# Full-array key-value products, TensorE transposes of one batch, and a new instruction order in a gated-linear-attention and MLP-mixer kernel

## The chip, the cores and the metric

The kernel runs on one core of a Trainium2 chip. A core has TensorE (PE in the profile; its weight loads are listed apart as PEld), VectorE (DVE), ScalarE (ACT), GpSimd (POOL) and SyncE (SP, which here only issues DMAs). TensorE writes into PSUM, which has eight banks; SBUF holds all other tiles. The metric is device time in microseconds of one execution, and the comparison is between medians of runs.

## What is computed

Four batches, eight heads, 768 tokens, 48 channels per head. First a recurrent linear attention with a decay per channel, then an MLP mixer over tokens and channels (384 channels, that is 8 x 48):

```python
for t in range(S):
    state = alpha[:, :, t, :, None] * state + np.einsum('bhd,bhe->bhde', k[:, :, t], v[:, :, t])
    y[:, :, t] = np.einsum('bhd,bhde->bhe', q[:, :, t], state)
...
xt = x.transpose(0, 2, 1)
h = np.maximum(xt @ w_tok1, 0.0) @ w_tok2
u = x + h.transpose(0, 2, 1)
h2 = np.maximum(u @ w_ch1, 0.0) @ w_ch2
return (u + h2).astype(np.float32)
```

Here x is y with the heads laid side by side: 768 tokens by 384 channels per batch.

## The kernel before

**Attention in chunks.** `attention(n)` (L126) handles one chunk of 256 tokens of one batch, for all eight heads; n runs from 0 to 11, and n = 3b + k is chunk k of batch b. A chunk's tokens lie as 128 partitions by two neighbouring tokens (the index s). Four loads of 384 KB bring alpha, k, q and v (`ld_at`, `ld_kt`, `ld_qt`, `ld_vt`, L138 to L142). Logarithms of alpha (ln, ln1, lnP; ACT) are summed over tokens on PE (cum, or cumw for the first three chunks) and turned into factors E and IE by exponentials (ACT). kk and qq (L170, L172) scale k and q by them into bf16 tiles pkk and pkq; vb (L174) casts v. For n of 3 and more, P, k0a, q0r and r1 first fold the two tokens of a partition.

trk and trq transpose pkk and pkq on PE (n below 6; copied out of PSUM by evk and evq), or dk and dq do it by DMA transposes issued on SP (n from 6), with pq reordering the result. G0 and G1 (`gmm`, L657) are the masked products of keys and queries inside each half chunk, 16 small products each on 48 rows by 64 columns of the array; mask0 and mask1 (DVE) bring them out. Half hf means the tokens on partitions 64 hf to 64 hf + 63.

**K.** The key-value product K (L205, `kmm`, L678) gives, for each half chunk, the sum over its tokens of key times value, for all heads. It works on 64 x 64 quarters of the array: for each pair of heads j, each s, each half hf and each head r of the pair, one product of 64 tokens with 48 moving columns; the two s accumulate in PSUM. That is 32 products, or 16 for the last chunk of a batch (k = 2), whose second half state nobody needs. The result holds one head of a pair in partitions 0 to 63 and the other in 64 to 127. `sfirst`, `sadd` (sa0, sa1) and `smul` (sm0, sm1) turn it into the running state, reading it twice (`twice`, L692) against a factor that is zero off the block diagonal. After K, vs0 and vs1 (`vswap`, L674) write v of the other token over the other half's partitions in vb, so that afterwards vb[:, hf] holds all 128 tokens of half hf. ia and ib (`inter`) then multiply q with the state before, y0 and y1 (`ymm`) add the products inside the half, and x0 and x1 copy the result to x tiles.

**Mixer.** `mixer(b)` (L247) runs once all six x tiles of a batch are there: t1 (`tok1`, two banks of six products; for batch 0 product by product as x tiles come, for the others six at a time, L254 to L264), ht (ReLU), t2 (`tok2`), u (add, DVE), the transposition of u, c1 (`ch1`, 24 steps of three products of 384 columns), rt (ReLU, on ACT or DVE), c2 (`ch2`, six tiles of 12 products in four steps), o (add u, DVE) and st (store). u is transposed by PE for batch 0 (up and ut, L281 to L289) and by two DMA transposes on SP for the other batches (ux, L290 to L296). The weights come in 16 pieces of 384 KB (`ldw_`), and each is cast to bf16 (`cw_`): wt1 and wt2 in two pieces each, wc1 and wc2 in six each. A c1 step of mc 6 to 11 needs pieces 3 to 5 of wc1, one of mc 0 to 5 needs pieces 0 to 2.

**The order.** Nothing is scheduled at run time by the kernel itself. `ORDER` (L337) lists every operation once, by name, with a last letter for its engine (t PE, s ACT, v DVE, g POOL, y SP); each engine works through its own in that order, and each waits for what it needs. `BUFS` gives the buffer number of each value, `CLASSES` (L103) the number of buffers of each kind. The cost figures and due times in `build` (L113) do not enter the program. Operations marked port=True on DVE and POOL wait for each other in the listed order where the engine changes (`shared`, L641). Loads may be issued from SP's queue or from ACT's, in turn with that engine's other work. The names f1_ and f3_ are fillers: one or three products of zeros of 512 columns (`fill`, L565), which are there only for the first three chunks.

Of the kernel before, what the change touches and what calls it, by code (L numbers as in the profile page):

```python
# [63 lines left out]
class Plan:  # L64
# [33 lines left out]
NX = 6  # L98
OFF = -1024.0
# [5 lines left out]
    "la": 2, "lf": 2, "E": 2, "IE": 2, "pkq": 2, "pkk": 2, "vb": 3,  # L105
    "tpk": 4, "tpq": 2, "gtm": 2, "tmp": 2, "ss": 5, "x": 12, "ht": 3, "u": 4, "ut": 2, "rt": 22, "o": 3,
# [6 lines left out]
def build(g):  # L113
# [12 lines left out]
    def attention(n):  # L126
# [70 lines left out]
        for hf in range(2):  # L197
# [7 lines left out]
        KO = O("K", {"PE": (276.0 if nst == 2 else 140.0, 420.0)}, 9.5, writes=[kp], reads=[pkk, vb], preds=[kk, vc] + fill("K", kp) + ([prev_s[1]] if prev_s and k > 0 and n > NB else []),  # L205
               emit=lambda e: g.kmm(kp, pkk, vb, nst), mode="G")
        before = prev_s if k > 0 else None
        states = [before]
        for hf in range(nst):
            s_, sp = V("ss"), states[-1]  # L210
            if sp is None:
                so = O(f"s{hf}_", dve(384), 10, writes=[s_], reads=[kp, E], preds=[KO, et],
                       emit=lambda e, s_=s_, hf=hf: g.sfirst(s_, kp, E, hf, wide))
            else:
                t_ = V("tmp")
                ad = O(f"sa{hf}_", dve(384), 10 + hf, writes=[t_], reads=[kp, sp[0]], preds=[KO, sp[1]],
                       emit=lambda e, t_=t_, hf=hf, s0=sp[0]: g.sadd(t_, kp, s0, hf))
# [3 lines left out]
        for hf, st in enumerate(states[:2]):  # L221
            yp, x = V("one"), V("x")
            vs = O(f"vs{hf}_", either(dve(384, True), act(384, True), {"POOL": (405.0, 440.0)}), 10, writes=[vb], reads=[vt],
                   port=True, preds=[KO, vc], emit=lambda e, hf=hf: g.vswap(e, vb, vt, hf))
            held = []
            if st:
                held.append(O(f"i{'ab'[hf]}", pe([96] * 4), 13, writes=[yp], reads=[tpq, st[0]], preds=[evq, st[1]],
                              emit=lambda e, hf=hf, st=st, yp=yp: g.inter(yp, tpq, st[0], hf)))
            yo = O(f"y{hf}_", pe([48] * 8), 14, writes=[yp], reads=[gtm, vb],
                   preds=[masks[hf], vs] + held + (fill("y", yp) if hf else []),  # L230
# [16 lines left out]
    def mixer(b):  # L247
# [4 lines left out]
        for m in range(NDT):  # L252
            bank, ht = V("one"), V("ht")
            if b == 0:  # L254
                prev = None
                for kc in range(NS):
                    o = P.op(f"t1_{b}_{m}_{kc}", pe([384]), m0 + 900 * m * sc + kc, writes=[bank], reads=[x[kc][0]],
                             preds=[x[kc][1], wl[("wt1", kc // 3)]] + ([prev] if prev else []),
                             emit=lambda e, m=m, kc=kc, bank=bank: g.tok1(bank, m, kc, x[kc][0]))
                    prev = o  # L260
            else:
                prev = P.op(f"t1_{b}_{m}", pe([384] * 6), m0 + 900 * m * sc, writes=[bank], reads=[v for v, _ in x],
                            preds=[o for _, o in x] + [wl[("wt1", p)] for p in range(2)],
                            emit=lambda e, m=m, bank=bank: [g.tok1(bank, m, kc, x[kc][0]) for kc in range(NS)])  # L264
            ho = P.op(f"ht_{b}_{m}", either(act(384), dve(384)), m0 + 1000 * m * sc, writes=[ht], reads=[bank],
                      preds=[prev], emit=lambda e, bank=bank, ht=ht: g.relu(e, g.hts(ht), bank))
            hts.append((ht, ho))
# [13 lines left out]
        if b == 0:  # L281
# [15 lines left out]
        for mc in range(NDC):  # L297
            rt = V("rt")
            ro = []
            for half in range(2):  # L300
                bank = V("one")
                o = P.op(f"c1_{b}_{mc}_{half}", pe([384] * 3), m0 + (4900 + 975 * mc + 487 * half) * sc, writes=[bank],
                         reads=[ut], preds=(uts[0:2 + half] if b == 0 else [uts[half]]) + [wl[("wc1", mc // 6 * 3 + p)] for p in range(3)],
# [5 lines left out]
        for i in range(NS):  # L309
            hold = 4000.0 if (i >= NS - 3 and b < B - 1) else 0.0  # L310
            bank, o_ = V("one"), V("o")
            prev = None
            for q4 in range(4):
                pp = []
                for mc in range(3 * q4, 3 * q4 + 3):
                    pp.append(rts[mc][1][i // 3])
                prev = P.op(f"c2_{b}_{i}_{q4}", pe([384] * 3), m0 + (16700 + 1950 * i + 487 * q4) * sc + hold,
                            writes=[bank], reads=[rts[mc][0] for mc in range(3 * q4, 3 * q4 + 3)],
                            preds=pp + [wl[("wc2", mc // 2)] for mc in range(3 * q4, 3 * q4 + 3, 2)] + ([prev] if prev else []),
                            emit=lambda e, i=i, q4=q4, bank=bank: g.ch2(bank, i, q4, rts))  # L320
            oo = P.op(f"o_{b}_{i}", dve(384), m0 + (16750 + 1950 * (i + 1)) * sc + hold, writes=[o_],
                      reads=[bank, us[i][0]], preds=[prev],
                      emit=lambda e, i=i, bank=bank, o_=o_: g.oadd(o_, bank, us[i][0], i))
            P.op(f"st_{b}_{i}", {"SP": (420.0, 420.0), "ACT": (374.0, 374.0)}, m0 + (16800 + 1950 * (i + 1)) * sc + hold, reads=[o_], preds=[oo],
                 emit=lambda e, i=i, o_=o_: g.store(e, o_, b, i), dma=("o", OUT_NS, 1000.0, 520.0))
# [15 lines left out]
ld_kt0s ld_at0y ld_vt0s ld_at1y f1_trq0t ld_kt1s ld_qt0y f3_cumw1t ld_qt1y f1_K0t f1_cumw0t f3_cumw0t f1_cumw1t  # L341
f3_trk0t ln0s ld_at2y ld_vt1s cumw0t f3_K0t IE0s f3_trq0t ln1s kk0g ld_at3s ld_kt2y cumw1t E0s Et0s IE1s qq0v trk0t
ldw_wt10y E1s evk0s ld_qt2s Et1s kk1v trq0t ld_kt3y f3_cumw2t vb0v evq0v qq1g K0t f3_trq1t vs0_0s vb1s s0_0v f1_G00t
ld_qt3y G0_0t sa1_0v f1_trq1t f1_trk1t vs1_0g mask0_0v sm1_0g ld_vt2s K1t ln2s trq1t trk1t P3g sa0_1v evq1s f1_G10t
# [483 lines left out]
```

## Time and profile before

| | |
|---|---|
| median of 3 runs | 169.35 us (168.55 to 169.62) |
| the profiled execution | 168.55 us |
| its span | 166.8 us |
| PE busy in the span | 158.8 us |
| DVE, ACT, POOL busy | 118.5, 88.8, 63.9 us |
| granted TensorE clock, mean | 0.997 |
| HBM read, written | 25.17 MB, 4.72 MB |

The profile is of one execution. A busy PE counts the whole passage of a product through the array, and products overlap; the distance from one product's start to the next is the better price of it. "Idle before" is time in which an engine waited, with the operation that released it. Times in a timeline count from the start of the span.

### The profile page before, as it was taken

The page shows a single profiled execution, that of the slowest core. Times are in us where ns is not written, and L with a number is a line of the kernel's source. Part 1 is how long each engine was busy: PE and PEld are TensorE (multiplying, and loading weights), DVE is VectorE, ACT ScalarE, POOL GpSimd, SP SyncE. Part 2 cuts the span into 40 slices and gives each one's busy share as a digit, 9 for nine tenths or more (in the row PEclk, how much of TensorE's full clock was granted, in tenths as well). Part 3 has the DMA queues.
Part 4 walks back from the last instruction along what each step waited for, and adds up shares of the span by engine and source line. Part 5 has one row for each costly group of instructions (what it writes and reads, how often), then busy time and mean ns, then how long its engine had stood idle before and what let it go on. Part 6 is the DMA issues. An engine that isn't in the chain of part 4 may idle for free.

```text
span 166.8 us, 4619 instructions
## 1 busy us (share of the span) xinstructions
PE 158.8 (95%) x1906; PEld 98.2 (59%) x1906; DVE 118.5 (71%) x208; ACT 88.8 (53%) x170; POOL 63.9 (38%) x68
## 2 busy tenths in 40 slices
PE   7969999889999999999899999999999999999991
PEld 2446565656566676565566676666566665665660
DVE  4059979889898869996998899892588463153522
ACT  3586978988678886735764842428602101641100
POOL 4139476296445661521646739436320000000000
PEclk9999999999999999999999999999999999999998
DMA  5999999999999999899999999489201186200213
GB/s 121 325 325 327 334 356 297 354 363 336 356 367 323 311 325 247 216 251 239 206 200 273 237 271 150 99 212 211 64 0 51 47 68 171 94 0 0 94 51 141
DMA packets 76757, 35.10 MB, mean 210 GB/s; under 512 B 70336, under 2 KB 75712, under 8 KB 76736
## 3 DMA queue, kind: packets, MB, share of 16 engines
q1 hardware_dynamic: 53168, 23.99, 58.5%
q10 hardware_dynamic: 23568, 10.82, 23.4%
q8 instruction: 15, 0.25, 0.7%
q14 instruction: 6, 0.05, 0.1%
HBM read 25.17 MB, written 4.72 MB: 179 GB/s over the span
## 4 chain that ended last, share of the span: by engine, by line
PE 76%; DMA 8%; DVE 6%; ACT 4%; issue 2%; SPq 1%; POOL 1%; DVEq 0%; ACTq 0%
PE ps L770 27%; PE ps L765 25%; PE ps L563 16%; DMA in<-in_q_dram 8%; PE ps L746 3%; PE ps L741 3%; PE ps L624 2%; DVE pkk L612 1%; ACT vb L654 1%; DVE o L774 1%; POOL tpq L655 1%; ACT tpq L654 1%; SPq L504 1%; DVE in L548 1%; DVE in L604 1%
## 5 line engine op out<-in xcount | busy, mean ns | idle before, releaser
L770 PE MATMUL ps<-wc,rt 128*128 128x384 bf16 x288 | 54.2, 326 | 0.1
L765 PE MATMUL ps<-ut,wc 128*128 128x384 bf16 x288 | 50.7, 326 | 0.7 <-DVE o L774 0.7
L736 ACT ACTIVATE rt<-ps 128x384 bf16<-128x384 f32 x52 | 23.5, 491 | 27.8 <-PE ps L765 27.6
L765 PEld LDWEIGHTS <-wc 128*128 128x128 bf16 x288 | 27.2, 98 | 18.4 <-issue 1.2
L770 PEld LDWEIGHTS <-rt 128*128 128x128 bf16 x288 | 26.7, 98 | 16.9 <-issue 0.3
L738 DVE TENSOR_SCALAR rt<-ps 128x384 bf16<-128x384 f32 x44 | 22.8, 551 | 15.5 <-PE ps L765 15.5
L670 DVE TENSOR_TENSOR gtm<-ps,mk 128x1024 bf16<-128x1024 f32 x24 | 28.8, 1220 | 3.6 <-PE ps L563 3.4
L774 DVE TENSOR_TENSOR o<-ps,u 128x384 f32<-128x384 f32 x24 | 13.1, 552 | 7.5 <-PE ps L770 7.4
L612 POOL TENSOR_TENSOR pkq<-in,E 128x768 bf16<-128x768 f32 x7 | 12.7, 1814 | 13.2 <-DVE in L608 7.1
L612 POOL TENSOR_TENSOR pkk<-in,IE 128x768 bf16<-128x768 f32 x7 | 12.7, 1814 | 10.7 <-ACT IE L596 5.2
L563 PE MATMUL ps<-zs 128*128 128x512 bf16 x51 | 15.5, 428 | 1.1 <-DVE zs L468 1.1
L654 ACT CAST vb<-in 64x384 bf16<-64x384 f32 (+1 forms) x24 | 14.5, 603 | 2.7 <-PE ps L563 2.0
L654 ACT CAST x<-ps 128x384 bf16<-128x384 f32 x18 | 8.3, 480 | 13.8 <-PE ps L563 12.6
L750 DVE TENSOR_TENSOR u<-ps,x 128x384 bf16<-128x384 f32 x24 | 12.4, 552 | 3.2 <-PE ps L746 3.1
L707 POOL TENSOR_TENSOR ss<-tmp,E 128x384 bf16<-128x384 f32 x10 | 8.4, 836 | 7.7 <-DVE vb L655 2.4
L703 DVE TENSOR_TENSOR tmp<-ps,ss 128x384 f32<-128x384 f32 x16 | 8.8, 552 | 1.9 <-PE ps L563 1.2
L746 PE MATMUL ps<-ht,wt 128*128 128x384 bf16 x48 | 9.8, 326 | 0.4 <-ACT ht L736 0.4
L612 DVE TENSOR_TENSOR pkq<-in,E 128x768 bf16<-128x768 f32 x5 | 4.8, 953 | 7.2 <-DMA in<-in_q_dram 7.1
L563 PEld LDWEIGHTS <-tpk 48*64 48x64 bf16 x384 | 6.3, 106 | 6.1 <-issue 4.9
L741 PE MATMUL ps<-x,wt 128*128 128x384 bf16 x48 | 9.6, 327 | 0.0
L563 PE MATMUL ps<-tpq,tpk 48*64 48x128 bf16 x384 | 9.1, 220 | 0.4 <-DVE u L750 0.2
L655 POOL COPY tpq<-tpk 128x1024 bf16<-128x1024 bf16 x5 | 6.7, 1339 | 5.8 <-PE ps L770 2.7
(85 smaller groups left out, 191.6 us busy)
## 6 DMA issues: line engine op xcount, KB each, us to landing
in<-in_moe_w_ch_dram SPq DMA_DIRECT2D x12, 384.0 KB, 6.4
in<-in_q_dram SPq DMA_DIRECT2D x10, 384.0 KB, 7.3
in<-in_alpha_dram SPq DMA_DIRECT2D x9, 384.0 KB, 6.5
in<-in_v_dram ACTq DMA_DIRECT2D x9, 384.0 KB, 6.3
in<-in_k_dram ACTq DMA_DIRECT2D x7, 384.0 KB, 5.8
out_dram<-o SPq DMA_DIRECT2D x13, 192.0 KB, 4.2
out_dram<-o ACTq DMA_DIRECT2D x11, 192.0 KB, 1.9
in<-in_k_dram SPq DMA_DIRECT2D x5, 384.0 KB, 6.9
```

The costliest lines, as they stand in the source:

```text
L563: return self.pe.matmul(out, lhsT=lhsT, rhs=rhs, start=start, stop=stop, skip_group_check=True)
L612: self.shared(self.eng[e].tensor_tensor(self.t(dst)[:, :, :, 0:D], self.t(src).rearrange("p h s d -> p s h d"), bass.AP(tensor=f.tensor, o ...
L654: return self.act.copy(d, s)
L670: self.nc.vector.tensor_tensor(self.t(gtm)[:, hf, :, :], self.pair(gp).rearrange("p a (j t) -> p (a j) t", t=128), bass.AP(tensor=m.tensor ...
L736: self.act.activation(d, s, AF.Relu)
L738: self.nc.vector.tensor_scalar_max(d, s, 0.0)
L741: self.pe.matmul(self.bank(bank)[:, 0:HD], lhsT=self.wt1[:, kc, m * 128 : m * 128 + 128], rhs=self.t(x), start=(kc == 0), stop=(kc == NS - 1))
L746: self.pe.matmul(self.bank(bank)[:, 0:HD], lhsT=self.wt2[:, kc, i * 128 : i * 128 + 128], rhs=self.t(hts[kc]), start=(kc == 0), stop=(kc = ...
L750: self.nc.vector.tensor_tensor(self.t(u)[:, i % 3], self.bank(bank)[:, 0:HD], self.t(x), ALU.add)
L765: self.pe.matmul(self.bank(bank)[:, 0:HD], lhsT=self.wc1[:, kc, mc * 128 : mc * 128 + 128], rhs=self.t(ut)[:, 3 * half : 3 * half + 3, kc, ...
L770: self.pe.matmul(self.bank(bank)[:, 0:HD], lhsT=self.t(rts[mc][0])[:, i * 128 : i * 128 + 128], rhs=self.wc2[:, mc, :], start=(mc == 0), s ...
L774: self.nc.vector.tensor_tensor(self.t(o), self.bank(bank)[:, 0:HD], self.t(u)[:, i % 3], ALU.add)
```

## The change

For chunks 3 to 11 (batches 1 to 3) K works on the whole array: `kfull` makes one product per pair of heads and half, over all 128 tokens of the half, with 128 stationary columns (two heads of 64) and 96 moving columns. That needs both tokens' keys of a half in one tile, as vs0 and vs1 give it for v; vs0 and vs1 now run ahead of K, and `kturn` copies the keys: ka and kb fill a new tile kt for half 1 (from both tokens of partitions 64 to 127), kc overwrites partitions 64 to 127 of pkk's first token by the other token of half 0, after trk (or dk) has read it. A last chunk of a batch needs kc and vs0 alone. The result holds 96 columns per pair, so the state steps read it directly.

u of batch 1 goes through PE (`UP`), as for batch 0, and no longer through DMA transposes. The first token products are single steps for all batches. The last tile of the last batch (`LAST`) is worked, added and stored in two halves of 192 columns. Some kinds have more buffers (E, IE, pkk, the new kt) and some fewer (x, rt, ss). `ORDER` and `BUFS` are new throughout; the second half's y filler, if any, stands ahead of ib instead of y1. There are 34 filler products instead of 51.

```diff
+KFN = 3
+LAST = (3, 0)
+UP = (0, 1)
...
-    "la": 2, "lf": 2, "E": 2, "IE": 2, "pkq": 2, "pkk": 2, "vb": 3,
-    "tpk": 4, "tpq": 2, "gtm": 2, "tmp": 2, "ss": 5, "x": 12, "ht": 3, "u": 4, "ut": 2, "rt": 22, "o": 3,
+    "la": 2, "lf": 2, "E": 3, "IE": 3, "pkq": 2, "pkk": 3, "vb": 3,
+    "tpk": 4, "tpq": 2, "gtm": 2, "tmp": 2, "ss": 4, "kt": 1, "x": 9, "ht": 3, "u": 4, "ut": 2, "rt": 20, "o": 3,
...
+        turned = n >= KFN
+        if turned:
+            vs = [vsw(hf, [vc]) for hf in range(2)]
+            kx, kp_in = None, [kk, vc, vs[0]]
+            if nst == 2:
+                kx = V("kt")
+                ka = shift("ka", 9, [kx], [pkk], [kk], lambda e: g.kturn(e, kx, pkk, 0))
+                kb = shift("kb", 9, [kx], [pkk], [kk], lambda e: g.kturn(e, kx, pkk, 1))
+                kp_in += [ka, kb, vs[1]]
+            kc = shift("kc", 9, [pkk], [], [kk, trk if n < NX else evk] + ([ka] if nst == 2 else []),
+                       lambda e: g.kturn(e, None, pkk, 2))
+            KO = O("K", pe([96] * (4 * nst)), 9.5, writes=[kp], reads=[pkk, vb] + ([kx] if kx else []),
+                   preds=kp_in + [kc] + ([prev_s[1]] if prev_s and k > 0 and n > NB else []),
+                   emit=lambda e: g.kfull(kp, pkk, kx, vb, nst))
...
-        if b == 0:
+        if b in UP:
             for p in range(3):
...
+            cuts = [(0, HD // 2), (HD // 2, HD)] if (b, i) == LAST else [(0, HD)]
...
+    def kturn(self, e, kx, pkk, part):
+        k = self.t(pkk)
+        d, s = ((self.t(kx)[0:64] if kx else None, k[64:128, 0]), (self.t(kx)[64:128] if kx else None, k[64:128, 1]),
+                (k[64:128, 0], k[0:64, 1]))[part]
+        self.copy(e, d[:, :, 0:D], s[:, :, 0:D])
+
+    def kfull(self, kp, pkk, kx, vb, nst):
+        vv = self.t(vb)
+        for hf in range(nst):
+            kk = self.t(kx) if hf else self.t(pkk)[:, 0]
+            for j in range(4):
+                self.mm(self.bank(kp, hf)[:, 96 * j : 96 * j + 96], kk[:, 2 * j : 2 * j + 2, :],
+                        vv[:, hf, 2 * j : 2 * j + 2, :], j == 0, j == 3)
```

Of the new order, the beginning, and the places that the prediction speaks of (the start of the old one stands at L338):

```
ld_at1s ld_at0y ld_qt0s ld_kt0y f1_G00t f3_cumw1t ld_qt1y f1_cumw1t ld_vt1y ld_kt1y f3_G00t f3_cumw0t ln0s ld_vt0s
f1_trq1t ln1s cumw0t cumw1t Et0s IE0s f1_trq0t ld_vt3y E0s kk0v Et1s E1s qq0v IE1s qq1v trq0t ld_at2y f1_trk0t evq0s
trk0t vb0v ld_qt2y evk0v kk1g K0t ld_at3s s0_0v f3_K1t ld_kt2s ld_kt3y sa1_0v vs0_0s trq1t ldw_wt10y sm1_0g G0_0t
vs1_0s G1_0t vb3s f3_trk1t mask1_0v ld_vt2y vb1s trk1t mask0_0v vs1_3s K1t ln2s vs1_1g evq1s sa0_1v vs0_1v cumw2t
...
t1_0_1_5t cw_wt21g trq3t ht_0_0v ht_0_1s ldw_wc11s sa1_3v cw_wc14g t2_0_0t ldw_wc10s t2_0_1t u_0_0v evq3s ld_kt5s
t2_0_5t cw_wc13g ln14s t2_0_3t u_0_1v t2_0_2t u_0_3v P5g ld_qt4y up_0_0t t2_0_4t u_0_2v ld_at6y u_0_5v up_0_1t lnP5s
cw_wc12g ld_qt5y u_0_4v ut_0_0s G0_3t ib3t ut_0_1v up_0_2t cw_wc15g mask0_3v cum5t ut_0_2s G1_3t c1_0_9_0t k0a4v
c1_0_8_1t IE5s ln15s mask1_3v E5s kk4g c1_0_8_0t rt_0_9_0s c1_0_11_1t rt_0_8_0s c1_0_6_1t r15s rt_0_11_1v y0_3t
cw_wc11s rt_0_8_1v y1_3t cw_wc10g ldw_wc20y trk4t x1_3s ldw_wc21y c1_0_7_0t kb4g r14s ld_vt4y c1_0_1_0t sm1_3g evk4s
...
c1_0_1_1t qq5g kc4g rt_0_1_1s rt_0_5_1v P6g trq5t vs1_4s rt_0_5_0v ld_at9y ld_at7s evq5v cw_wc24s kc5g vs0_4g ld_qt6y
c1_0_6_0t c2_0_4_0t c1_0_10_1t ia4t c2_0_0_0t cw_wc22v rt_0_6_0s y0_4t K4t rt_0_10_1v cw_wc23s vb6v c2_0_1_0t cw_wc25s
...
t1_1_0_5t ht_1_1v dq6y c2_0_3_0t c2_0_5_3t ht_1_0s ld_kt8s q0r7g t2_1_3t ld_qt9y cum7t ld_vt8s u_1_3v t2_1_2t IE7s
```

## What is predicted

> **What bounds the kernel now.** I read the page's busy times and chain first, then busy time by stretches of 10 us, then TensorE's (PE's) timeline, where the distance from one start to the next is the price of a step, then DVE, ACT and the landings of loads.
>
> ```profile
> PE 158.8 (95%) x1906; PEld 98.2 (59%) x1906; DVE 118.5 (71%) x208; ACT 88.8 (53%) x170; POOL 63.9 (38%) x68
> PE 76%; DMA 8%; DVE 6%; ACT 4%; issue 2%; SPq 1%; POOL 1%; DVEq 0%; ACTq 0%
> ```
>
> ```profile
> 10.00:20.00 10.00, 9.12 (x186) 5.47 (x183) 9.54 (x13) 8.03 (x14) 5.02 (x6) 1.00 1.16 330
> 30.00:40.00 10.00, 8.72 (x123) 5.67 (x122) 8.85 (x17) 8.96 (x16) 6.02 (x7) 1.00 1.07 360
> 110.00:120.00 10.00, 10.00 (x70) 6.05 (x67) 4.71 (x11) 6.37 (x15) 3.89 (x4) 1.00 0.87 167
> ```
> (columns: PE, weight load, DVE, ACT, POOL, clock, DMA, GB/s). PE is the bound, but not everywhere alike: up to 40 us it is full of fillers while DVE, ACT and DMA are at 8 to 10 tenths; later its work is real. The seam is the first channel product, c1, at 37.88, which follows the last u transposes taken out of PSUM:
>
> ```profile
> 36.66 1.08 DVE L655 COPY ut<-ps 128x768 bf16<-128x768 bf16 x2
> 37.88 1.30 PE L765 MATMUL ps<-ut,wc 128*128 128x384 bf16 x7
> ```
>
> From 37.88 to the end of the last product's turn, 163.23, PE's steps take 125.35 us. By usual start-to-start times (c1 and c2 0.4875 per three products, G 0.248, y 0.205, i 0.17, cum 0.29, transposes 0.445 per eight) 121.05 is work, 14 runs of quadrant steps cost 0.188 each = 2.65 beyond their work, and 1.65 is waiting: 0.28 at 67 us, 0.24 at 73 to 75, 0.90 at 79, 0.23 at 100. The largest:
>
> ```profile
> 78.07 1.14 PE L765 MATMUL ps<-ut,wc 128*128 128x384 bf16 x6
> 79.94 0.97 PE L765 MATMUL ps<-ut,wc 128*128 128x384 bf16 x5 [0.73 <-DVE o L774]
> ```
> ```profile
> 78.86 0.56 DVE L608 TENSOR_TENSOR in<-in,lf 128x384 f32<-128x384 f32 x1 [1.25 <-DMA in<-in_q_dram]
> ```
> DVE stood at q0r9, whose load was issued at 73.31 behind two DMA transposes of u on SP (ux, 1.39 and 1.40 us of issue) and landed at 78.77; the bank that c1 needed was freed behind it.
>
> **The sum, part by part.** It is made against the profiled execution: 168.55 us with a span of 166.8. It is the fastest of the three runs shown; the median, 169.35, is 0.8 above, so I add 0.8 at the end.
>
> *Key-value products.* The quadrant form and its surroundings:
>
> ```profile
> 50.44 0.65 PE L765 MATMUL ps<-ut,wc 128*128 128x384 bf16 x3
> 51.02 0.44 PE L563 MATMUL ps<-vb,pkk 64*64 64x48 bf16 x32
> 51.39 0.62 PE L624 MATMUL ps<-idn,pkk 128*128 128x128 bf16 x8
> ```
> ```profile
> 95.54 0.42 PE L563 MATMUL ps<-tpq,tpk 48*64 48x128 bf16 x16
> 95.79 0.42 PE L563 MATMUL ps<-vb,pkk 64*64 64x48 bf16 x32
> 96.04 0.43 PE L563 MATMUL ps<-tpq,tpk 48*64 48x128 bf16 x16
> ```
> Alone, K's 32 products take 0.37, and the three c1 ahead take 0.58, not 0.4875; between two G steps K takes 0.25. So a run of quadrant steps costs some 0.09 going in and 0.10 coming out, and K itself 0.27 (half of it 0.20, between 0.185 and 0.246). A full-array product of 96 columns is the i row: four in 0.17. New K: eight = 0.34, or four = 0.17. For K4 to K11 (five whole, three half) 2.21 replaces 1.95: +0.26. But runs after the first c1 go from 14 to 10 in the new order: -0.75. [...]
>
> *Copies.* 21 new half-tile copies; nearest rows:
>
> ```profile
> L654 ACT CAST vb<-in 64x384 bf16<-64x384 f32 x17 | 8.7, 510 | 2.7 <-PE ps L563 2.0 <-issue 0.4
> L655 POOL CAST vb<-in 64x384 bf16<-64x384 f32 x5 | 2.5, 501 | 7.2 <-DVE ss L707 4.0 <-DVE in L604 3.0
> L655 DVE CAST vb<-in 64x384 bf16<-64x384 f32 x2 | 0.7, 356 | 0.1
> ```
> 9 on ACT 4.6, 9 on POOL 4.5, 3 on DVE 1.1. Nothing of it is on PE, which hides it as long as K's place comes late enough. K now waits for them, and every product behind K on PE with it. The tightest is K4, just before c2_0_1_0: after q0r5 POOL has qq5 1.81, kc4 0.50, P6 1.00, kc5 0.50, vs0_4 0.50 = 4.3 us to do, and the order leaves 4.6 us of PE work for it. Price: 0 to 1, in the waits below.
>
> *u of batch 1 by TensorE.* 18 transposes, three steps of 0.345 = +1.03 on PE, all on the path. Three copies out (DVE 0.56 twice, ACT 0.82) lie beside products of c2_0. Gone are two DMA transposes and SP's 2.8 us. ld_qt9 moves ahead to t2_1, and q0r9 comes some 11 us of PE work later (before: 5.6), so the 0.90 and the 0.24 should go.
>
> *First token products by tile* add no instruction: 0; the 0.23 at 100 may go. *Halved last product*: 24 products of 192 columns for 12 of 384, about +0.02; the end shrinks by 0.08 in the last product and 0.20 in the last addition (0.552 for 384 columns; the 1024-column row 1.22 gives 1.04 ns a column). The store's 1.8 us from issue to landing I leave: -0.28, between 0 and -0.5. *Fewer buffers* (x, rt, ss): 0 to 1, in the waits below.
>
> *New order, start.* Fillers fall from 51 to 34; at 0.216 that is 3.7 us of PE, but they only filled waiting. What counts is when c1 can start. Three queues by rows:
> - DVE, from its first product to the last u copy: before 27.5 us of rows in 27.54 elapsed. New 28.4 (it takes kk0 and qq1 ahead and more x copies), but starts at about 8.0 instead of 10.19, since kt0 and qt0 are now second on each queue (before, second loads landed at 7.67 and 8.40) and IE0 is done at about 8.0: 36.4.
> - ACT, from its first Ln to the ut copy: before 28.9 of rows in 31.6. New 28.8, with the same 2.7 of gaps from 5.05: 36.5.
> - Weights: the last piece that the first c1 needs is the 26th load (before 25th). Landings 25 to 27 were 33.73, 34.74, 35.83; with the cast of 0.82 on POOL: 35.6 to 36.7.
>
> I take 36.5: -1.38. Ends 35.8 and 39. Two moves speak for the late end: vt3 is loaded ahead of at2, and its cast stands on ACT ahead of vb1, ln2 and evq1, so cumw2 comes late (the ninth load landed at 14.91; 0.83, 0.83, 0.51 and 0.84 behind it, some 0.1 overlapped each, give 17.6 for 16.79); and four of the six wc1 loads move from SP to ACT, in turn with its work. 0.33 of PE work (cum5, ib3, G1_3 for trq4) moves ahead of the seam: -0.33.
>
> After the seam: 121.05 + 2.65 + 0.26 - 0.75 + 1.03 + 0.02 - 0.33 = 123.93. New waits: 1.0, nearest the 1.65 of before less the 0.9 whose cause goes, between 0.2 and 4. PE ends at 36.5 + 123.93 + 1.0 = 161.43 for 163.23: -1.8; tail -0.28. 168.55 - 2.1 = 166.5, on the median's footing **167.3**.
>
> **Rivals.**
> - *Gain given back.* The order is tighter: copies ahead of K, fewer buffers, DVE 1.8 and ACT 7 us fuller over the kernel (rows times the counts in both orders). Waits of 2.5 to 3 instead of 1.0: 168.8 to 169.3. For it: DVE is at 9 tenths and more from 10 to 30 and 60 to 110 us. Against: K's result is needed steps later, and most copies stand several products ahead.
> - *PE goes cold in the start.* The first ten fillers took 427 ns each, later ones 216. With fewer fillers PE pauses for about 2 us near 8 to 10 us; if it went back to 427, work of some 2.4 us up to 16 us would double, and up to 1.2 would reach the seam: 168.5. Against: before it paused 0.81 at 10.4 and stayed at 216. [...]
> - *Slower: the wc1 loads on ACT come late.* wc11 and wc10 are issued on ACT behind ht_0_1 (31.73 in the trace), and wc10's cast stands on POOL behind kk4 (1.81). The seventh c1 product, c1_0_1_0, due at 40.2, needs both. A load takes 6.4 us to land at the median. From 2.1 us of waiting there nothing is gained any more: if ht_0_1 slips to 35, wc10 lands at 41.4, is cast by 42.3 to 44, and c1_0_1_0 waits 2.1 to 3.8; c2's weights, behind it in the same stream, cost another 1 as slack is gone: 170.4 to 172.1, say 171.3. Against: by the ACT rows ht_0_1 stands at 31 to 32.
> - *Better still*: seam at 35.8, waits 0.2: 165.8. For it: the wc15 load may be cast by 35.6. Against: DVE's rows end at 36.4.
>
> **Numbers.** Forecast 0.50 (166.4 to 168.1, of which 0.44 lies below 167.66), better still 0.08, given back 0.22, cold start 0.05, slower 0.15. About 1% is what a measurement of this kernel can tell from no change: 167.66 and 171.04. Faster 0.52, same 0.33, slower 0.15. The range leaves out a tenth at each end: 165.5 to 171.0.
>
> **What would show it.** Right: first c1 at 36 to 37; no wait at q0r9; K of 96 columns in 0.34 with no 0.58 step ahead of it; ten quadrant runs after the seam; waits on PE after it of about 1 us; the last addition at 0.35. Wrong: c1 beyond 38; PE idle ahead of K4 or another K, released by a POOL or ACT copy; fillers at 427 after 8 us.

## The result, and the profile after

| | before | after |
|---|---|---|
| median of 20 runs each | 169.2 us (167.48 to 170.81) | 171.16 us (168.9 to 173.75) |
| ratio of after to before | | 1.0103, 95% interval 1.0073 to 1.0134 |
| profiled execution, its span | 168.55, 166.8 us | 170.48, 168.8 us |
| granted clock, mean of the profiled execution | 0.997 | 0.990 |
| start of the first c1 product (the seam) | 37.88 us | 40.01 us |

The change is slower by 1.0%; 167.3 us was forecast. The ratio leaves out the executions that are over 1.5% longer than the shortest of their kernel (eight of the twenty after the change), so it is not the quotient of the two medians. The spans of the two profiled executions differ by 1.93 us before rounding, in three stretches: the seam is 2.13 later, the stretch from there to the end of the last product's turn 0.18 longer (125.53 for 125.35), the tail behind it 0.38 shorter (3.23 for 3.61).

The page of the changed kernel, with its busy times, the granted clock in 40 slices of 4.2 us, and the chain's share by engine and line:

```profile
PE 156.9 (93%) x1739; PEld 99.7 (59%) x1739; DVE 121.2 (72%) x214; ACT 95.1 (56%) x178; POOL 69.6 (41%) x81
PEclk9999879999999999999999999999999999999999
PE 76%; DVE 7%; DMA 5%; POOL 5%; issue 2%; ACT 2%; POOLq 0%; DVEq 0%
PE ps L815 28%; PE ps L810 21%; PE ps L592 17%; DMA in<-in_alpha_dram 5%; PE ps L791 4%; PE ps L786 3%; DVE pkq L641 2%; PE ps L653 1%; DVE u L795 1%; POOL in L637 1%; PE ps L802 1%; POOL pkq L641 1%; DVE rt L783 1%; POOL pkk L684 1%; ACT r
```

PE has less to do than before (156.9 for 158.8: fewer fillers), and yet the time is longer. Two things are new: one load of alpha makes up 5% of the chain (before, loads of q made up 8%), and the clock drops to 8 and 7 tenths in the fifth and sixth slice. The stretches of 10 us show where (columns as in the prediction):

```profile
10.00:20.00 10.00, 5.81 (x139) 4.38 (x140) 8.51 (x14) 6.22 (x9) 3.11 (x3) 0.99 1.17 325
20.00:30.00 10.00, 9.86 (x165) 6.47 (x163) 7.08 (x11) 8.73 (x16) 4.13 (x4) 0.84 1.00 309
30.00:40.00 10.00, 9.00 (x147) 5.93 (x144) 9.66 (x16) 7.55 (x12) 7.98 (x10) 1.00 0.92 293
```

From 10 to 20 us PE is busy for 5.81 us instead of 9.12 and ACT for 6.22 instead of 8.03: something is missing there for both. ACT's timeline names it, in brackets at the end of a line:

```profile
14.07 2.10 ACT L683 CAST vb<-in 128x768 bf16<-128x768 f32 x3 [0.59 <-DMA in<-in_v_dram]
18.48 0.84 ACT L586 ACTIVATE la<-in 128x768 bf16<-128x768 f32 x1 [2.31 <-DMA in<-in_alpha_dram]
```

and PE's timeline, behind K1:

```profile
15.69 0.44 PE L592 MATMUL ps<-vb,pkk 64*64 64x48 bf16 x32
19.38 0.72 PE L592 MATMUL ps<-la,u 128*128 128x384 bf16 x3 [3.25 <-ACT la L586]
```

In the kernel before, the same two rows, ln2 on ACT and cumw2 on PE, were these:

```profile
15.35 0.84 ACT L557 ACTIVATE la<-in 128x768 bf16<-128x768 f32 x1 [0.98 <-DMA in<-in_alpha_dram]
```
```profile
16.79 0.66 PE L563 MATMUL ps<-la,u 128*128 128x384 bf16 x3
```

The logarithm of chunk 2 (ln2) now waits 2.31 us for alpha, PE waits 3.25 us for ln2: cumw2 starts at 19.38 (before: 16.79), and from 19.82 to 23.23 the clock is half. The landings say why. ld_at2 was issued on SP at 9.78, behind ld_vt3 (7.86), and landed at 18.46; before, it was issued at 5.60 and landed at 14.91. ld_at3, issued 0.9 us later but on ACT's queue, landed at 15.24, ahead of it.

The seam itself, DVE's and PE's timelines of the changed kernel:

```profile
35.94 2.93 DVE L795 TENSOR_TENSOR u<-ps,x 128x384 bf16<-128x384 f32 x6 [0.21 <-PE ps L791]
38.78 0.55 DVE L684 COPY ut<-ps 128x768 bf16<-128x768 bf16 x1
```
```profile
38.96 0.50 PE L802 MATMUL ps<-idn,u 128*128 128x128 bf16 x6
39.29 0.33 PE L592 MATMUL ps<-la,u 128*128 128x384 bf16 x1
...
39.66 0.42 PE L592 MATMUL ps<-tpq,tpk 48*64 48x128 bf16 x16
40.01 1.31 PE L810 MATMUL ps<-ut,wc 128*128 128x384 bf16 x7
```

The copy that the first c1 product needs ends at 39.33; PE still has the rest of a transposition, cum5 and G1_3 to do, so 0.68 us pass.

Behind the seam the largest wait of the changed kernel is ahead of K7, for the copy kc7 on POOL:

```profile
84.60 0.34 PE L592 MATMUL ps<-vb,pkk 128*128 128x96 bf16 x4 [0.54 <-POOL pkk L684]
84.78 0.33 PE L592 MATMUL ps<-vb,kt 128*128 128x96 bf16 x4
84.95 1.30 PE L810 MATMUL ps<-ut,wc 128*128 128x384 bf16 x7
```

Eight products take 84.60 to 84.95, 0.35 us. By start-to-start times the waits after the seam are 0.71 ahead of K7, 0.29 behind K4 (ahead of c2_0_1_0), 0.26 at ib8 and 0.16 in two smaller places, 1.41 in all. q0r9's wait is gone.

### The profile page after: what moved, and what is told of

It reads as the page before. It is cut to its first block, busy times and chain, and to the rows that moved or that the text cites. A ratio compares the mean times of both kernels' runs of the same rounds, so it can differ in the third digit from the quotient of the medians.

```text
span 168.8 us, 4322 instructions
## 1 busy us (share of the span) xinstructions
PE 156.9 (93%) x1739; PEld 99.7 (59%) x1739; DVE 121.2 (72%) x214; ACT 95.1 (56%) x178; POOL 69.6 (41%) x81
## 4 chain that ended last, share of the span: by engine, by line
PE 76%; DVE 7%; DMA 5%; POOL 5%; issue 2%; ACT 2%; POOLq 0%; DVEq 0%
PE ps L815 28%; PE ps L810 21%; PE ps L592 17%; DMA in<-in_alpha_dram 5%; PE ps L791 4%; PE ps L786 3%; DVE pkq L641 2%; PE ps L653 1%; DVE u L795 1%; POOL in L637 1%; PE ps L802 1%; POOL pkq L641 1%; DVE rt L783 1%; POOL pkk L684 1%; ACT rt L781 1%
## 5 line engine op out<-in xcount | busy, mean ns | idle before, releaser
L815 PE MATMUL ps<-wc,rt 128*128 128x384 bf16 (+1 forms) x300 | 54.6, 320 | 0.1
L781 ACT ACTIVATE rt<-ps 128x384 bf16<-128x384 f32 x53 | 24.8, 493 | 30.1 <-PE ps L810 29.5
L819 DVE TENSOR_TENSOR o<-ps,u 128x384 f32<-128x384 f32 (+1 forms) x25 | 13.4, 538 | 15.2 <-PE ps L815 12.3
L641 POOL TENSOR_TENSOR pkk<-in,IE 128x768 bf16<-128x768 f32 x8 | 14.6, 1819 | 21.2 <-ACT vb L683 10.3
L592 PE MATMUL ps<-zs 128*128 128x512 bf16 x34 | 12.4, 492 | 1.2 <-DVE zs L495 1.1
L683 ACT CAST x<-ps 128x384 bf16<-128x384 f32 x13 | 6.3, 482 | 9.9 <-PE ps L592 9.3
L786 PE MATMUL ps<-x,wt 128*128 128x384 bf16 x48 | 10.6, 326 | 0.0
L592 PEld LDWEIGHTS <-gtm 128*128 128x128 bf16 x192 | 7.7, 97 | 2.2 <-DVE gtm L699 0.5
L592 PE MATMUL ps<-vb,gtm 128*128 128x48 bf16 x192 | 8.5, 185 | 0.1
L622 ACT ACTIVATE IE<-ps 128x384 f32<-128x384 f32 x9 | 4.4, 491 | 6.8 <-PE ps L592 6.7
L641 DVE TENSOR_TENSOR pkq<-in,E 128x768 bf16<-128x768 f32 x8 | 7.5, 954 | 1.0 <-POOL in L637 0.8
```

The costliest lines, as they stand in the source:

```text
L592: return self.pe.matmul(out, lhsT=lhsT, rhs=rhs, start=start, stop=stop, skip_group_check=True)
L641: self.shared(self.eng[e].tensor_tensor(self.t(dst)[:, :, :, 0:D], self.t(src).rearrange("p h s d -> p s h d"), bass.AP(tensor=f.tensor, o ...
L683: return self.act.copy(d, s)
L781: self.act.activation(d, s, AF.Relu)
L786: self.pe.matmul(self.bank(bank)[:, 0:HD], lhsT=self.wt1[:, kc, m * 128 : m * 128 + 128], rhs=self.t(x), start=(kc == 0), stop=(kc == NS - 1))
L815: self.pe.matmul(self.bank(bank)[:, 0 : cz - ca], lhsT=self.t(rts[mc][0])[:, i * 128 : i * 128 + 128], rhs=self.wc2[:, mc, ca:cz], start=( ...
```

## The experiments

Each kernel was run beside the kernel before, and its ratio is against those runs. Seam and waits are those of one profiled execution. "Work" is PE's time from the first c1 product to the start of the last product, less the waits in it.

| kernel | cumw2 | half clock, us | seam | waits after | work after | ratio (95%) |
|---|---|---|---|---|---|---|
| before | 16.79 | none | 37.88 | 1.61 | 123.26 | 1 |
| after | 19.38 | 19.8-23.2 | 40.01 | 1.41 | 123.88 | 1.0103 (1.0073-1.0134) |
| e1_warm | 20.86 | 10.9-17.7 | 40.08 | 3.23 | 123.87 | 1.0172 (1.0114-1.0230) |
| e4_actlate | 17.48 | 10.6-14.0 | 38.61 | 1.93 | 123.93 | 1.0087 (1.0047-1.0127) |
| e7_warm2 | 19.51 | none | 38.96 | 2.33 | 123.96 | 1.0103 (1.0042-1.0165) |
| e8_at2 | 16.87 | none | 38.27 | 2.49 | 123.94 | 1.0116 (1.0049-1.0183) |
| e9_swap | 21.91 | 19.0-25.8 | 42.79 | 3.03 | 123.88 | 1.0336 (1.0258-1.0413) |
| e12_vt3late | 19.24 | 10.2-17.0 | 40.66 | 2.02 | 123.89 | 1.0118 (1.0086-1.0149) |
| e13_best | 16.94 | 29.4-32.8 | 39.16 | 1.28 | 123.83 | 1.0020 (0.9991-1.0049) |
| e16_best2 | 16.84 | none | 37.95 | 2.15 | 123.84 | 1.0074 (1.0051-1.0097) |
| e5_blate | 20.25 | 19.5-26.3 | 43.54 | 2.10 | 123.25 | 1.0259 (1.0193-1.0326) |
| e15_blwarm | 20.03 | none | 40.75 | 2.66 | 123.27 | 1.0159 (1.0125-1.0193) |
| e14_up2 | 17.01 | none | 37.85 | 3.66 | 124.40 | 1.0069 (1.0033-1.0104) |

A trace is one execution, and not always a usual one: those of e1_warm, e5_blate and e14_up2 are the longest of their kernel's runs, those of e8_at2 and e16_best2 the shortest. Four versions (e14_up2, e6_up, e17_two, e18_two2) leave the start of the kernel before as it is, and their seams lie between 37.45 and 37.85, that of the kernel before at 37.88. So a difference of up to 0.4 us between the seams of two traces is not shown to come from an edit. The median of the kernel before, too, lay between 168.76 and 169.72 us in the eight comparisons.

The theory that I set out with: alpha of chunk 2 is late because of its place in the loads, and all that follows is late with it. Its rivals: the half clock costs the time, whatever the load does; or DVE, fuller than before, sets the end of the start.

**Is the late load enough?** In the kernel before, only its place was changed:

```diff
-ln0s ld_at2y ld_vt1s cumw0t f3_K0t IE0s f3_trq0t ln1s kk0g ld_at3s ld_kt2y cumw1t
+ln0s ld_vt1s cumw0t f3_K0t IE0s f3_trq0t ln1s kk0g ld_at3s ld_kt2y ld_at2y cumw1t
```

> The kernel before with nothing but the load of chunk 2's alpha moved later on SP, behind k of chunk 2. Late-alpha theory: alpha lands at 17.5 to 19, the sum of chunk 2 begins at about 19 to 19.5 in place of 16.79, the first c1 product 1.5 to 2.5 us later than 37.88, ratio 1.008 to 1.016. Rival, that the start of the kernel before has slack there and only the changed kernel's own work makes the delay count: the first c1 product by 38.4, ratio 1.003 or less.

Measured: alpha landed at 19.34, ln2 stood 4.91 us for it, the seam came 5.66 us later, more than either theory said. ACT in this run:

```profile
19.36 0.84 ACT L560 ACTIVATE la<-in 128x768 bf16<-128x768 f32 x1 [4.91 <-DMA in<-in_alpha_dram]
```

One load moved by one place on SP costs 2.6%, which is 4.4 us; the 5.66 are of the longest of the four runs. The clock was half from 19.5 to 26.3, so the two causes had to be parted, by 13 fillers in PE's idle time:

```diff
-G1_0t sm0_1g cumw2t
+G1_0t sm0_1g f13_cumw2t cumw2t
```

> The kernel before with the load of chunk 2's alpha moved behind k of chunk 2, as in the earlier run of that move, and 13 filler products in the idle time ahead of the sum of chunk 2. Theory that the half clock from 19.5 to 26.3 made up the rest of that run's 5.7 us: alpha still lands at about 19.3 and the sum begins at about 20.2, the clock stays at 1.00, the first c1 product at 40.5 to 41.5 in place of 43.5, ratio 1.012 to 1.020. Rival, that the late alpha alone cost it: the first c1 product at 43 or later, ratio 1.024 or more.

Measured: alpha at 18.80, cumw2 at 20.03, no half clock, seam at 40.75, ratio 1.0159. So in the kernel before a load that lands 3.9 us later costs 2.9 us of the seam, and the half clock behind PE's wait (3.33 us in e5_blate, filled in e15_blwarm) up to 2.8 more (by the two ratios 1.7; alpha also landed 0.5 later in e5_blate). The late load costs time by itself, and so does the half clock behind it; that the late load alone cost it is ruled out.

**How much of it is the clock in the changed kernel?** The first try put 12 fillers only ahead of cumw2.

```diff
-sa0_1v vs0_1v cumw2t
+sa0_1v vs0_1v f12_cumw2t cumw2t
```

> The changed kernel with twelve more filler products between K1 and cumw2 (2.6 us of PE, which stood idle there from 16.0 to 19.4), nothing else. Late-alpha theory (the changed kernel's start is late because chunk 2's alpha lands at 18.46, and the fall of the clock is only its consequence): cumw2 still starts at 19.3 to 19.5, the clock stays at 1.0, the seam (first c1) moves from 40.0 to 39.3 to 39.8, ratio to before 1.006 to 1.009. Cold-clock rival (the missing fillers let the clock fall to half from 19.8 to 23.2, and that is what made the start late): seam at 38.3 or earlier, ratio 1.000 or less. Full-DVE rival: no move of the seam beyond 0.2, ratio 1.008 to 1.012.

Measured: no answer. In this execution PE had already been idle from 8.1 to 9.8, the clock was half from 10.9 to 17.7, so K1 started at 17.88 (15.69 in the changed kernel). The 12 fillers behind it took 0.216 us each and ended at 20.86, when ln2 had long been done; that is where cumw2 starts. The second try put fillers into PE's pauses from 8 us on as well:

```diff
-IE0s f1_trq0t ld_vt3y
+IE0s f9_trq0t ld_vt3y
-kk1g K0t
+kk1g f3_K0t K0t
-sa0_1v vs0_1v cumw2t
+sa0_1v vs0_1v f12_cumw2t cumw2t
```

> The changed kernel with more of the filler products that the start already has (nine ahead of the first q transpose in place of one, three ahead of the first key-value product, twelve ahead of the sum of chunk 2's logarithm), so that PE is never idle for long in the start; the loads are as in the changed kernel, alpha of chunk 2 lands as late. Late-alpha theory: the granted clock stays near 1.00 through the start, the sum of chunk 2 still begins at about 19.4 us, the first c1 product at 39.3 to 39.8 (before 37.88, changed kernel 40.01), ratio to the kernel before 1.004 to 1.009. Rival, that the half clock from 19.8 to 23.2 us cost the time: the first c1 product at 38.3 or earlier, ratio 1.000 or less.

Measured: clock 1.00 throughout, alpha as late as ever (18.59), cumw2 at 19.51, seam at 38.96. The value lies between the two ranges: the half clock had cost 1.05 of the 2.13 us by which the changed kernel's seam is later than before, and the other half stays as long as alpha is late. But the ratio did not move (1.0103), above both ranges, and in this execution a new wait took the microsecond back. PE stood 1.08 us ahead of ib8, released by POOL's scaling of the state, and the reason is on DVE:

```profile
99.18 0.56 DVE L822 TENSOR_TENSOR o<-ps,u 128x384 f32<-128x384 f32 x1 [1.32 <-DMA out_dram<-o]
```

DVE waited for the buffer of an output tile: the store of batch 0's first tile was issued on ACT at 93.86 and landed at 99.16, against 94.92 and 99.24 in the changed kernel. The landing stayed where it was, so a start that is 1.05 us earlier only waits 0.99 us longer at ib8 (1.25 for 0.26). Why the store lands no earlier stays open.

**Does alpha land late because of the other queue?** ACT's two loads were moved behind vb1:

```diff
-K0t ld_at3s s0_0v f3_K1t ld_kt2s
+K0t s0_0v f3_K1t
-ld_vt2y vb1s
+ld_vt2y vb1s ld_at3s ld_kt2s
```

> The changed kernel with the loads of chunk 3's alpha and chunk 2's k, issued on ACT at 10.7 and 11.1, moved behind vb1 on ACT (about 14.8); SP's loads keep their order. If ACT's queue took the bandwidth from SP's queue while at2 was next: at2 lands at 15.3 to 16.5 instead of 18.46, cumw2 starts at 16.5 to 17.6, seam at 37.8 to 39, ratio 0.995 to 1.004. If at2 is late only by its place behind the v load: at2 lands after 17.5, seam at 39.5 or later, ratio 1.006 or more.

Measured: ld_at2, issued at 9.74 as before, landed at 15.28 instead of 18.46, cumw2 at 17.48, seam at 38.61 in spite of a half clock from 10.6 to 14.0. Loads on the other queue, issued after it, had cost it 3.2 us. The ratio, 1.0087, lies with the other answer all the same. ACT's row of ln2, no longer waiting for the load, and PE's of cumw2, which now waits for a mask on DVE:

```profile
16.15 0.84 ACT L589 ACTIVATE la<-in 128x768 bf16<-128x768 f32 x1
```
```profile
17.48 0.66 PE L595 MATMUL ps<-la,u 128*128 128x384 bf16 x3 [0.90 <-DVE gtm L702]
```

How one queue's loads hold up the other's was not shown; the traces have the landings alone. In the changed kernel ld_at3, issued at 10.69 on ACT, landed at 15.24, 3.2 us ahead of ld_at2, which had been issued 0.9 earlier on SP.

**Is it the place of the load or ACT's order?** Two runs exchanged ld_at2 and ld_vt3 on SP. Their first versions, e2_at2 and e3_swap, kept alpha's old buffer, so that alpha of chunk 2 was written over k of chunk 0 before kk0 had read it, and kk0 waited for it and scaled the wrong numbers; ratios of 1.0553 and 1.0492 tell nothing of the question. The second versions give alpha a free buffer:

```diff
-f1_trq0t ld_vt3y E0s kk0v Et1s E1s qq0v IE1s qq1v trq0t ld_at2y
+f1_trq0t ld_at2y E0s kk0v Et1s E1s qq0v IE1s qq1v trq0t ld_vt3y
```

> The changed kernel with the two loads exchanged and alpha of chunk 2 in a buffer of its own, as in the run beside it, but with the cast of v of chunk 3 left where it stands on ACT, ahead of v of chunk 1, the logarithm of chunk 2 and the copy of q1. Theory that load place and order on ACT go together: v of chunk 3 now lands at about 18.4 us, ACT stands at its cast, the sum of chunk 2 begins at 19.8 to 21, the first c1 product at 40 to 41, ratio 1.009 to 1.018. Rival, that the place of the load alone decides: as the run beside it, 0.988 to 0.998.

Measured: as the theory said, and worse: v of chunk 3 landed at 18.87, and ACT, where its cast stands first, waited 5.56 us with alpha long landed (13.94):

```profile
18.89 2.10 ACT L686 CAST vb<-in 128x768 bf16<-128x768 f32 x3 [5.56 <-DMA in<-in_v_dram]
```

In e8_at2 the cast and the scales are moved as well:

```diff
-G1_0t vb3s f3_trk1t
+G1_0t f3_trk1t
-mask0_0v vs1_3s K1t
+mask0_0v K1t
-y1_0t vs0_3v G0_1t r13s
+y1_0t G0_1t r13s vb3s vs1_3s
-mask0_1v sm1_1g
+mask0_1v vs0_3v sm1_1g
```

> The changed kernel with alpha of chunk 2 issued where v of chunk 3 stood on SP and v of chunk 3 where alpha stood, alpha in a buffer of its own that nothing else uses so early, and the cast and scale of v of chunk 3 moved behind chunk 2's work on ACT (one scale on DVE). Late-alpha theory: alpha lands at about 14 us, the sum of chunk 2 begins at 17 or earlier, the first c1 product at 37.0 to 38.2, ratio 0.988 to 0.998. Rival, that DVE, fuller in the start by the transposed u and the masks, holds the end of the start whatever the logarithm does: the first c1 product at 39.3 or later, ratio 1.005 or more.

Measured: alpha at 14.10, cumw2 at 16.87, which is the time of the kernel before, no half clock. Yet the seam is at 38.27, just past the theory's range, and the ratio is 1.0116, well outside it and in the rival's. DVE's wait for the store's buffer grew to 1.48 us. The profiled execution, 169.9 us, is also the shortest of its runs (169.9 to 173.4): its mean clock is 1.00, as in one other (170.1), while the four with 0.98 took 171.4 to 173.4. So in four of the six the clock fell by its mean, and the trace shows one in which it did not.

**What holds the start then?** e12_vt3late loads v of chunk 3 much later and moves its rows behind chunk 2's. (A first version, e10_vt3late, and e11_best on top of it, loaded it into a buffer that alpha of chunk 5 filled before v's scales were made, so that these copied the wrong numbers; 1.0461 and 1.0406 tell nothing.) At their old places, left out here, the moved names go.

```diff
-f1_trq0t ld_vt3y
+f1_trq0t ld_at2y
-ld_vt2y vb1s
+ld_vt2y ld_vt3y vb1s
-ka3s sa0_2v
+ka3s vb3s sa0_2v
-mask1_2v sm0_2g
+mask1_2v vs0_3v sm0_2g
-kb3s lnP4s
+kb3s vs1_3s lnP4s
```

> The changed kernel with alpha of chunk 2 loaded where v of chunk 3 stood and the load of v of chunk 3 put behind that of v of chunk 2 on SP, each into a buffer that nothing else holds at that time; the cast and one scale of v of chunk 3 stand behind k of chunk 3 on ACT, the other scale behind a mask of chunk 2 on DVE. Theory that the end of the start is set by which loads and which rows on ACT stand ahead of chunk 2's logarithm and exponentials: alpha lands at about 14, the first c1 product at 36.7 to 37.5 (40.01 in the changed kernel, 38.27 with v of chunk 3 only moved behind alpha); after it 126.4 us to PE's end, with waits of 2.5 in them, ratio 0.986 to 0.997. Rival, that the start can't be shorter than about 38.2 because DVE's own rows fill it: the first c1 product at 38.0 or later, ratio 0.998 to 1.008.

Measured: seam 40.66, and a ratio of 1.0118, above both ranges for it, but with the clock half from 10.2 to 17.0, so this one decides nothing. e13_best adds fillers at 8 us, one scale on DVE instead of POOL, and takes away two waits behind the seam:

```diff
-f1_trq0t ld_at2y
+f9_trq0t ld_at2y
-kk1g K0t
+kk1g f3_K0t K0t
-sm1_1g
+sm1_1v
-r19s
+r19s st_0_0s
-ka7v q0r9v
+ka7v kc7v q0r9v
-vs1_7s kc7g
+vs1_7s
-kk10g st_0_0s
+kk10g
```

> The run beside it with four more moves: the copy for K7 made by DVE right behind its partner instead of on POOL, the store of batch 0's first result issued on ACT some 23 us earlier, one scale of the state of chunk 1 on DVE instead of POOL, and nine and three filler products ahead of the first q transpose and the first key-value product. Theory: the wait ahead of K7 (0.7) and the one behind DVE's wait for the store's buffer (1.4) are gone, K4's 0.28 stays: the first c1 product at 36.3 to 37.2, after it 124.0 to 124.7, ratio 0.975 to 0.985. Rival, that such waits only move to the next late step: after the first c1 product 125.5 or more, ratio 0.988 or more.

Measured: ratio 1.0020 (0.9991 to 1.0049), no difference from the kernel before that can be told, and seam 39.16; both lie far above the theory's ranges. The store's wait is gone. K7's copy is early, but K7 waits as long as before, now for its second bank, which DVE's rt copy empties:

```profile
83.09 0.33 PE L595 MATMUL ps<-vb,pkk 128*128 128x96 bf16 x4
84.00 0.34 PE L595 MATMUL ps<-vb,kt 128*128 128x96 bf16 x4 [0.58 <-DVE rt L786]
```

In the start the scale that I had moved on DVE held POOL up, PE stood still for 1.66 us behind it, and the clock was half from there to 32.84. e16_best2 mends both:

```diff
-mask1_2v vs0_3v sm0_2g
+mask1_2v sm0_2g
-kb3s vs1_3s lnP4s
+kb3s lnP4s vs1_3s vs0_3s
-K7t P11v c1_1_5_0t rt_1_7_0s rt_1_7_1s k0a8g rt_1_5_1s c1_1_6_1t
+P11v c1_1_5_0t rt_1_7_0s rt_1_7_1s k0a8g rt_1_5_1s c1_1_6_1t K7t
-K4t rt_0_10_1v cw_wc23s vb6v c2_0_1_0t
+rt_0_10_1v cw_wc23s vb6v c2_0_1_0t K4t
```

> The run with four more moves, mended where its trace showed new waits: the scale of v of chunk 3 made by ACT behind its partner instead of DVE (on DVE it held POOL's scale of the state of chunk 2 until 28.67, PE stood still 1.5 us and the clock was half from 29.4 to 32.8), K7's products two c1 products later (they waited 0.75 for a bank that DVE's rt copy freed) and K4's one c2 product later. Theory: the clock stays 1.00 in the start, the first c1 product at 36.8 to 37.6, after it 124.0 to 124.6 to PE's end (waits under 0.8), ratio 0.980 to 0.991. Rival, that the next late row holds the start again: the first c1 product at 38.3 or later, ratio 0.995 or more.

Measured: clock 1.00, seam 37.95, between the two ranges, ratio 1.0074, in the rival's. This is the best start that any version of the changed kernel had, though the trace is of the shortest of twelve runs, and it is that of the kernel before. This run (stretches of 10 us):

```profile
20.00:30.00 10.00, 9.32 (x174) 6.27 (x173) 9.98 (x14) 9.76 (x17) 5.76 (x7) 1.00 1.04 319
```

DVE is busy for 9.98 of 10 us and ACT for 9.76: with alpha in time, these two engines' own rows fill this stretch, which speaks for the rival. Which of the two ends the start is not shown: the first c1 product also needs a copy of u that ACT makes, the first of the two in this row, and it ends at 37.55, later than DVE's at 37.06:

```profile
36.77 1.48 ACT L686 COPY ut<-ps 128x768 bf16<-128x768 bf16 x2
```

And K7's wait has moved once more, to a c1 product ahead of it, with the same releaser:

```profile
84.00 0.65 PE L813 MATMUL ps<-ut,wc 128*128 128x384 bf16 x3 [0.75 <-DVE rt L786]
84.48 0.33 PE L595 MATMUL ps<-vb,pkk 128*128 128x96 bf16 x4
```

By the two traces e16_best2's last product starts 0.33 us earlier than e13_best's (163.94 for 164.27), yet its ratio is higher. The medians are 169.82 and 169.60; most of the difference in the ratio is that of the kernel before in the two comparisons (168.91 and 169.40).

**Single parts on the kernel before.** First u of batch 1 by TensorE alone:

```diff
-        if b == 0:
+        if b in (0, 1):
...
-lnP9s ux_1_1y ld_at11s
+lnP9s ld_at11s
-u_1_1v sm1_6g vb8s c2_0_0_1t k0a9v o_0_5v ux_1_0y c2_0_0_2t
+u_1_1v up_1_2t sm1_6g vb8s ut_1_2s c2_0_0_1t up_1_1t ut_1_1v k0a9v o_0_5v c2_0_0_2t up_1_0t ut_1_0s
```

> The kernel before with u of batch 1 transposed by TensorE and nothing else of the change, once more for a profile: its time stood at 1.0102 of before, above what the terms gave. Theory: the added products cost what was reckoned (1.03 us in the row of 335 ns for six), and the 0.9 us wait in batch 1's c1 products is either still there or replaced by one of the same size behind the added copies on ACT and DVE. Rival: the work added is larger, 1.8 us or more.

Measured: work 124.40, that is +1.14 for the 1.03 reckoned. The same kernel as e6_up had the ratio 1.0102 (1.0051 to 1.0152); its profiled execution was by far the longest of its runs (173.2 us, the others 170.2 to 171.2) and is read only for its start. The trace read here is the longest of its eight runs, too (171.6, median 170.3). The 0.90 at c1_1_2_0 is gone, but waits sum to 3.66, among them 1.36 ahead of c2_0_3_0, where DVE had stood 1.08 us for a load of alpha. Then the halved last tile and the load of q9 ahead of the two ux:

```diff
-lnP9s ux_1_1y ld_at11s
+lnP9s ld_qt9y ux_1_1y ld_at11s
-cum9t ld_qt9y K7t
+cum9t K7t
-c2_3_0_0t c2_3_1_0t
+c2_3_0h1_0t c2_3_0h0_0t c2_3_1_0t
...
```

> The kernel before with two small parts alone: the last tile of the last batch in two halves of 192 columns, as in the change, and the load of q9 on SP moved ahead of the two DMA transposes of batch 1's u. Theory that these are the parts whose terms held: the end behind the last product's turn is 0.28 to 0.35 shorter, q0r9 on DVE no longer waits for its load and the 0.90 in batch 1's c1 products goes, the rest as before: ratio 0.991 to 0.995. Rival, that the wait moves, since the transposes of u now start behind a load and land later, and the c1 products of batch 1 wait for them: ratio 0.997 to 1.003.

> The kernel before with the halved last tile and the earlier load of q9, once more for a profile: the profiled execution of the first look was at the upper end of its own runs (170.9 of 167.9 to 170.9). Theory: in an execution near the median the 0.90 ahead of c1_1_2_0 is gone and no wait of its size takes its place, waits after the first c1 product sum to 0.8 or less (1.61 before), the end is 0.28 to 0.35 shorter, ratio 0.992 to 0.996. Rival: a wait of 0.6 or more stands ahead of K7 or a c1 product of batch 1 in its place, ratio 0.997 or more.

Measured, the same kernel twice: 0.9967 (0.9930 to 1.0004) and 0.9982 (0.9946 to 1.0017), no difference that can be told. In e18_two2 the wait at q9 is gone, but its waits after the seam sum to some 3.3 us, not 0.8 or less; 1.36 us of them stand ahead of c2_0_3_0, again behind DVE's wait for alpha (0.99), as in e14_up2, where q9's load had not moved. So that place is not shown to follow from the move; what makes that load land late in some executions stays open. The second half's o buffer was also one still being stored, which spends the tail's gain here.

## Why the prediction was wrong, point by point

- **The seam: 36.5 forecast, 40.01 measured.** This step failed, the term "New order, start" with its -1.38, and it made 3.5 of the 4.0 us by which the profiled execution (170.48) lies above the forecast on its footing (166.5); waits made 0.4, the work 0.2, and the tail gave 0.1 back. The runs part the 3.5, one profiled execution each: 1.05 half clock (after to e7_warm2), 0.69 late alpha without it (to e8_at2), 0.32 what e16_best2 changes further (v of chunk 3's rows, a scale on POOL, more fillers). This last part is within the 0.4 by which equal starts differ. The remaining 1.45 no version reached.
- **The late alpha was seen and mis-sized.** The text gave cumw2 17.6 for v of chunk 3, the ninth load, landing at 14.91, and ACT's four rows behind it. That load landed at 14.05. But ln2 needs the tenth, alpha, and the text gave that no landing time of its own: at3, issued after it on ACT, came first, and it landed at 18.46. cumw2 started at 19.38. The text named this and still let it cost nothing at the seam, which stayed at 36.5.
- **The queues: DVE's ends at 36.4 by the text, 39.33 in the changed kernel, 37.06 at best** (e16_best2). There it starts with kk0 at 8.42, not 8.0 (0.42; with the same order up to there it starts at 7.8 to 8.4 in the traces), takes 28.64 instead of 28.4 (0.24), and 0.89 pass from its copy to the first c1 product instead of 0.1 (0.79): together the 1.45. In those 0.89 ACT's copy of u ends at 37.55, by the text's row of ACT 36.5, and cum5 and G1_3 stand ahead on PE. The text had moved those steps ahead of the seam for a gain of 0.33 and let them cost nothing there.
- **The cold clock was a rival with 0.05.** It came, and not as a rare case. In the kernel before the mean clock was 0.996 or more in all but two of the 113 executions that have it on record (0.99 in those two); in the twenty of the changed kernel it was 0.97 to 0.99, and 3.41 us at half clock take 0.01 off the mean over 168.8 us. In the profiled execution the fall came at 19.8, behind PE's wait for the late logarithm, and none came behind the pause at 7.9 to 10.0 (PE's work is 2.12 us from 6.17 to 9.58 and 2.15 from 9.58 to 13.00, both at 1.00). In e1_warm, e4_actlate and e12_vt3late, whose PE work is the same up to there, it came at 10.2 to 10.9, behind that very pause, as the rival said. Why the clock falls behind this pause in one execution and not in another was not shown (e9_swap, with 1.64 us of work from 8.77 to 12.18, kept its clock there). What the text had against it, fillers that stayed at 216 ns behind a pause of 0.81, says little of one of 2.1. And late load and cold clock were reckoned as independent; in e5_blate the moved load alone came with a half clock from 19.5 to 26.3, where the kernel before had none.
- **The work after the seam: right.** 123.93 forecast to the end of the last turn. That is 123.69 to the last start (its turn is half of 0.4875); 123.88 was measured, and 123.83 to 123.96 in all nine versions of the changed kernel in the table. The ten quadrant runs, K in 0.35, and the transposed u (1.14 for 1.03, alone) bear the terms out. To the end of the last turn that is 124.12 against 123.75 before: no gain, 0.37 more where the text had 0.23 more.
- **Waits: 1.0 forecast, 1.41 measured.** The 0.90 and the 0.24 went, as said; 0.71 came ahead of K7, as the list of signs had it ("another K released by a POOL or ACT copy"), and 0.29 behind K4. K4 itself did not wait: the last of the copies priced for it ended at 55.40, and K4 started at 55.89, right behind y0_4. Take one wait away and another takes its place: with an earlier start there are 2.33 in e7_warm2, 2.49 in e8_at2 and 2.15 in e16_best2. That is the rival "gain given back", which cost little in the changed kernel while its start was late. The line for it, DVE at 9 tenths and more from 60 to 110 us and from 10 to 30, was read too high: the stretches at 20, 70 and 90 us have 8.65, 8.26 and 8.58 of 10.
- **Tail: -0.38 for -0.28.** The last addition takes 0.36.
- **wc1 loads on ACT late:** no c1 product waited over 0.1 us for a weight in the changed kernel, but this is in part luck. ht_0_1 stood at 34.45, not at 31 to 32; the cast of wc10 ended at 43.73, 0.24 ahead of c1_0_1_0, and with the seam where the text had it that product was due at 40.2. In e16_best2 the cast came at 41.47 and the product at 41.81.

Two thirds of the forecast gain was the seam, -1.38 of 2.1; the rest was waits and the tail, less 0.2 of work. As DVE's rows are 1.7 us longer than before up to the last needed copy (26.4 busy for 24.8, overlaps taken out) and begin 1.8 earlier in e16_best2, the start could stand still by them; that it could not get shorter with another order is argued, not shown. No version of the changed kernel beat the kernel before; e13_best cannot be told from it (1.0020) and beat the changed kernel's ratio. What sets the time of these versions beyond the start, the waits that move, was not settled.

## What to carry to other kernels

Price a moved load by its landing, and a landing by all queues together: what is issued later on another queue can land first (in the changed kernel 0.9 us later, and 3.2 ahead). Where an engine's queue is full to nine tenths (here DVE and ACT, 9.98 and 9.76 of 10 us in e16_best2), count its rows with what the order puts between its last row and the step that waits; a gain that rests on it finishing earlier needs rows taken away, not moved. An idle stretch on PE costs twice if the clock falls behind it (2.9 us of the seam in e15_blwarm, up to 2.8 more in e5_blate), so price the two together, and read the clock of every execution, not of the profiled one alone.

## What the runs showed of the hardware

In seven of the traces the granted clock fell to half in the start. It stayed there for 3.41 us in the changed kernel, e4_actlate and e13_best, and for 6.82 to 6.83 in e1_warm, e5_blate, e9_swap and e12_vt3late. PE was not always idle ahead of a fall; it also came behind 3.41 us in which PE was busy for half of the time. In the changed kernel (first column the stretch, as long as the shorter falls, then its length and PE's busy time; clock in the third column from the end):

```profile
13.00:16.41 3.41, 3.04 (x85) 2.18 (x83) 2.56 (x4) 2.56 (x4) 2.67 (x3) 1.00 1.17 326
16.41:19.82 3.41, 0.44 (x3) 0.39 (x4) 3.30 (x8) 1.34 (x2) 0.45 (x1) 1.00 1.16 321
19.82:23.23 3.41, 3.41 (x44) 2.08 (x42) 1.33 (x2) 3.07 (x6) 0.83 (x1) 0.50 1.06 304
```

and in e13_best:

```profile
26.02:29.43 3.41, 1.73 (x45) 1.28 (x45) 3.33 (x6) 3.35 (x6) 2.08 (x3) 1.00 1.08 371
29.43:32.84 3.41, 3.29 (x38) 2.42 (x38) 2.14 (x4) 1.76 (x5) 2.35 (x4) 0.50 1.08 374
```

Over the seven falls the 3.41 us ahead held 0.00 (e9_swap) to 1.81 us (e12_vt3late) of PE's work. But busy time alone does not draw the line: in e9_swap a stretch with 1.64 was not followed by a fall:

```profile
8.77:12.18 3.41, 1.64 (x49) 1.43 (x49) 2.71 (x4) 2.50 (x3) 0.00 (x0) 1.00 1.17 325
12.18:15.59 3.41, 3.11 (x65) 2.12 (x55) 2.55 (x5) 1.02 (x2) 2.60 (x2) 1.00 1.19 329
```

What makes the clock fall was not shown. In e13_best 1.73 us of work in the stretch, with 1.66 us of idleness in one piece, went with a fall. In the changed kernel a filler took 0.426 us from its start to the next one's at half clock (from 22.63), and 0.216 at full clock (from 23.53).
